# Sparse attention and feed-forward layer on one core: batch 1's K and Q in whole rows, batch 2 by natural loads and the crossbar, x of three batches by the crossbar

## The chip, the cores and the metric

The kernel runs on one core of a Trainium2 chip. The metric is the device time of one execution in microseconds (us). The core has TensorE (PE in the profile), VectorE (DVE), ScalarE (ACT), GpSimd (POOL) and SyncE (SP), which work beside each other and wait on semaphores, and 16 DMA engines that all transfers share.

## The reference

Attention over 4 batches, 8 heads, 768 positions and a head size of 64, with a band of 16 positions to each side and 24 summary keys (the maximum of each block of 32 keys, whose value is the block's mean), and then a feed-forward layer:

```python
k_sum = k.reshape(B, H, nb, block, D).max(axis=3)        # block = 32
v_sum = v.reshape(B, H, nb, block, D).mean(axis=3)
mask_l = np.abs(pos[:, None] - pos[None, :]) < window    # window = 16
scores_l = scale * (q @ k^T), -1e9 where not mask_l
scores_s = scale * (q @ k_sum^T) + np.log(block)
a = softmax(concat([scores_l, scores_s]))
x = (a @ concat([v, v_sum])).transpose(0, 2, 1, 3).reshape(3072, 512)
h = x @ w_in                                             # 512 x 2048
out = (h * np.clip(h + 3.0, 0.0, 6.0) / 6.0) @ w_out     # 2048 x 512
```

## The kernel before

The work is written as several hundred small operations, each with a tag, a number and an engine. `ORDER` is a text that lists all of them (`F30.0` is operation 0 of tag `F30`; `:A` or `:D` puts it on ACT or DVE where either can do it). A planner (`Plan.run`) goes through the text, gives each operation a begin from costs and due times written beside it, and the program is issued in the order of these begins. Within one engine that is the order of the text. On the chip each engine takes its operations strictly in that order and waits for what they need.

The tags: `K`, `Q`, `V` are loads that POOL issues (first digit the batch), `I` and `O` the parts of w_in and w_out, `h` the halo of V (the neighbouring 32 rows), `B` loads of V in blocks and `U` their sums on DVE. `k` and `q` bring K and Q into a layout with the head's 64 numbers across partitions, `w` makes the summary keys and the keys' halo, `s` is scores (matmuls on PE, the exponential on ACT, the mask's product on DVE), `u` block sums of V and their spreading, `v` the values. `v` with batch and 0 or 3 is one half of a batch: two groups of 24 small matmuls, a reciprocal and a product on DVE each, and then x turned so that the model dimension is across partitions. Half a batch is a tile s = 2b + half of 384 rows. `F` with tile and group is the first feed-forward product, 16 columns of 128 (operations 0 and 1 are four matmuls of 384 columns each, 2 is ACT's part, 3 DVE's); `G` with tile and 128-row part is the second product in four pieces of four matmuls of 512 columns, then a copy to `ot` and a store. Tile 0 is F0 and G0, and so on to 7. The halves of a batch come in the order 1, 0, so tile 3 goes ahead of tile 2.

Loads and turns before the change:

- Batch 0 has a path of its own, which the change leaves alone.
- Batches 1 and 2 (`load_raw`, line 450): K and Q come in 8 DMAs of 192 KB (in bf16) each, in which 32 of a head's 64 numbers go to one group of 32 partitions, so that each piece is half a row. `turn_raw` (608) turns them by 32x32 blocks on DVE, four operations for K and four for Q, into a layout with one head on 64 partitions. V's block sums come from matmuls (`vsum`, 745).
- Batch 3 (`load_nat`, 436): K and Q come in 12 natural loads of 128 rows (two of which are split in two DMAs) and are turned by four DMA transposes, the crossbar, issued by SP (`k_turn` 598, `q_turn` 589). V comes a second time in blocks (`load_blocks`, 727) and DVE sums it (`sum_blocks`, 732).
- Scores of batches 1 to 3 (`scores_all`, 666): six passes of 16 matmuls, each on 64 of the 128 rows, two heads at a time side by side.
- x (`values_half`, 825): tiles 2, 4, 5, 6 and 7 by the crossbar on SP; tile 3 (batch 1's half 1) by 12 PE transposes and three copies. After tile 2's turn POOL reads one number of it (`y10.0`, line 858), so that no load is issued before it has landed. Some F pieces of tile 3 are cut into thirds (`FINE`).
- Stores (`f2`, 941): SP issues them, except those of tile 5's part 1, which POOL issues.

A DMA that SP or POOL issues stands in that engine's queue behind what was listed before it, waits included. Buffers tie the steps: raw or natural K and Q of batches 2 lie in `both[0]`, those of 1 and 3 in `both[1]`; batch 3's V blocks lie in `both[0]`, so their loads wait until batch 2's K and Q have been turned. There are four `ot` buffers.

Of the kernel before, what the change touches and what calls it, by code (L numbers as in the profile page):

```python
# [12 lines left out]
F32 = mybir.dt.float32  # L13
# [5 lines left out]
D = 64  # L19
# [31 lines left out]
G12.4:A F33.4 G12.5 F30.7 F31.6 F33.5 y10.0 G01.5 F33.6 k21.0 F31.7 F33.0 F33.7 F33.1 h20.0 G31.0 Q32.0 F33.2 V30.0 F32.0  # L51
k20.0 F31.0 F33.3 F31.1 F31.2 k22.0 F32.1 F32.4 k23.0 F32.2 F32.5 F31.3 q23.0 G32.0 F32.6 Q33.0 F20.0 w2.3:A F32.3 F32.7
F20.1 G31.1 F20.2 G32.1 G32.2 F20.3 F21.0 q21.0 F21.4 q20.0 w2.4:A F21.5 F21.1 F20.4 w2.0 F21.6 F21.2 G31.2 G32.3 q22.0 V20.0
F20.5 G32.4:A F21.7 F20.6 F23.0 F23.1 w2.1 G31.3 w2.2:A F20.7 V22.0 G30.0 F21.3 h22.0 G30.1 F23.2 K31.0 s240.0 F23.3 s230.0
s250.0 G30.2 h30.0 G31.4:A s240.1 F22.0 F22.1 B33.0 G30.3 s250.1 s230.1 F22.2 V21.0 u2.0 q24.0:A s210.0 s220.0 F22.3 s200.0
G30.4:A s210.1 s240.2 s220.1 u2.1:D u2.8:D s250.2 s210.2 u2.2:D u2.9:A u2.4:A s230.2 s220.2 u2.7:D G20.0 F22.4 F22.5 F22.6
F23.4 G22.0 F23.5 G20.1 G22.1 F22.7 u2.3:D u2.6:D F23.6 F23.7 s200.1 v20.0 v20.3 s200.2 v20.4 v20.1 u2.5:D v20.2 v20.5 B31.0
K32.0 Q35.0 h31.0 K35.0 K33.0 Q31.0 V32.0 K34.0 B32.0 B30.0 h32.0 V31.0 Q34.0 Q30.0 V33.0 G21.0 G21.1 G22.2 G22.3 v23.3 v23.0
G20.2 G20.3 G21.2 G21.3 v20.6 G30.5 G21.4:A U3.2 v23.1 v23.4 U3.3 v23.2 U3.0 v23.5 F40.0 F40.1 F40.2 F41.4 F41.5 F41.6 F40.3
F41.7 G00.5 v23.6 q3x0.0 F41.0 F41.1 F41.2 F41.3 F42.0 F42.1 F42.2 G20.4:A F42.3 F40.4 F40.5 F40.6 F40.7 k3e0.0 G21.5 G32.5  # L60
# [12 lines left out]
G62.4:D G62.5 G71.2 G71.5 G71.8 G71.15 G71.16:A G71.17
# [199 lines left out]
def kernel(  # L273
# [42 lines left out]
    qs = {1: q1, 2: q2}  # L316
# [6 lines left out]
    raw = [{n: t[:, i * NS:(i + 1) * NS].rearrange("p u m -> p (u m)").rearrange("p (y c) -> p y c", c=BLK) for i, n in enumerate("KQ")} for t in both]  # L323
# [112 lines left out]
    def load_nat(b, name, u):  # L436

        plan.at(f"{name}{b}{u}")
        src, shift = (k, 0) if name == "K" else (q, PAD)
        n, lo = shift if u == 0 else 0, 128 * u - shift  # L440

        def go():
            o = nat[b % 2][name][:, u].rearrange("p (h d) -> p h d", h=H)
            if n:
                nc.gpsimd.dma_start(out=o[0:n], in_=src[b, :, S - n:S].rearrange("h r d -> r h d"))
            nc.gpsimd.dma_start(out=o[n:128], in_=src[b, :, lo + n:lo + 128].rearrange("h r d -> r h d"))
        op("POOL", 1.4 if n else 0.9, go, over=0.01, w=[(name + "n", b % 2, u)], dma=0.88, els=1024,
           free=[(name + "r", 1, g) for g in range(4)])

    def load_raw(b):  # L450
        for name, src in (("K", k), ("Q", q)):
            for g in range(4):
                plan.at(f"{name}{b}{g}")
                hs, ds, rows = slice(4 * (g // 2), 4 * (g // 2) + 4), slice(BLK * (g % 2), BLK * (g % 2) + BLK), slice(BLK * g, BLK * g + BLK)
                op("POOL", 1.35, over=0.01, fn=lambda src=src, name=name, hs=hs, ds=ds, rows=rows: nc.gpsimd.dma_start(  # L455
                    out=raw[b % 2][name][rows], in_=src[b, hs].rearrange("h (c r) d -> r (h c) d", r=BLK)[:, :, ds]),
# [640 lines left out]
```

## Time and profile before

| | us |
|---|---|
| median of 3 runs | 212.12 (211.94 to 213.3) |
| the profiled execution | 211.65 |
| its span, first to last instruction | 209.9 |
| PE busy | 201.7 |
| DVE busy | 156.0 |
| ACT busy | 110.8 |
| POOL busy | 68.9 |

The profile is of one execution. PE is matmuls and PEld weight loads, which overlap them. A view groups instructions by line, engine and operation: busy time, then the mean duration of one in ns, then the engine's idle time before them and what ended it. The chain of waits is followed back from the last instruction; its pieces have a start, a length and what they were. A stretch is a window of the span with each engine's busy time. The times to landing are from a DMA's issue to the end of its transfer.

### The profile page before, as it was taken

The numbers are of one execution on the slowest core, as the hardware profiler recorded it, in microseconds if no ns is written. First come the engines' busy times: TensorE is split into PE (matmuls) and PEld (weight loads), VectorE is DVE, ScalarE is ACT, GpSimd is POOL, SyncE is SP. The second block draws the span as 40 slices with busy tenths as digits, with TensorE's granted clock in tenths as the row PEclk, the third lists the DMA queues.
The fourth block names the chain that finished last, engine by engine and source line by source line (L and its number), as shares of the span: only waits on it lengthen the run. The fifth ranks groups of instructions, "written<-read, shape, count | busy, mean of one in ns | idle before, by whom it ended". The sixth has DMA issues, their size and how long they took to land.

```text
span 209.9 us, 5030 instructions
## 1 busy us (share of the span) xinstructions
PE 201.7 (96%) x2143; PEld 119.1 (57%) x2166; DVE 156.0 (74%) x229; ACT 110.8 (53%) x158; POOL 68.9 (33%) x89
## 2 busy tenths in 40 slices
PE   8999999999999999999999999999999999999993
PEld 2667876554455787455655466554554565665442
DVE  6898968997969989797599977899473756543212
ACT  5788576654389574547880166451990445623000
POOL 7572489626735603989840000000000100000000
PEclk9999999999999999999999999999999999999999
DMA  6999999999999999999995679900016310001055
GB/s 143 198 160 189 165 152 131 204 135 152 158 159 157 124 110 199 137 164 160 161 169 38 173 132 208 214 24 0 2 54 174 67 61 0 3 0 62 23 185 182
DMA packets 117638, 25.85 MB, mean 123 GB/s; under 512 B 108368, under 2 KB 114320, under 8 KB 117616
## 3 DMA queue, kind: packets, MB, share of 16 engines
q0 software_dynamic: 99488, 15.47, 106.8%
q1 hardware_dynamic: 18128, 10.06, 20.3%
q8 instruction: 17, 0.28, 0.6%
q14 instruction: 5, 0.04, 0.1%
HBM read 30.75 MB, written 6.29 MB: 176 GB/s over the span
## 4 chain that ended last, share of the span: by engine, by line
PE 60%; DMA 22%; POOL 5%; issue 5%; DVE 5%; ACT 2%; SPq 0%; POOLq 0%; ACTq 0%
PE S L928 28%; PE h L950 19%; PE S L950 9%; DMA vaug<-in_v_dram 9%; DMA wout<-in_moe_w_out_dram 5%; DMA win<-in_moe_w_in_dram 4%; DMA g<-in_q_dram 3%; PE S L841 2%; POOL nat L455 2%; DMA out_dram<-ot 2%; DVE at L689 2%; DVE g L936 1%; PE S L681 1%; DVE vaug L517 1%; ACT at L687 1%
## 5 line engine op out<-in xcount | busy, mean ns | idle before, releaser
L928 PE MATMUL S<-x,win 128*128 128x384 bf16 (+1 forms) x616 | 87.8, 299 | 0.4 <-ACT ot L517 0.3
L936 DVE SCALAR_TENSOR_TENSOR g<-r,S 128x768 bf16<-128x768 f32 x64 | 59.9, 948 | 24.5 <-ACT r L934 24.2
L934 ACT ACTIVATE r<-S 128x768 f32<-128x768 f32 x64 | 51.1, 810 | 46.0 <-PE S L928 42.0
L928 PEld LDWEIGHTS <-win 128*128 128x128 bf16 x616 | 53.6, 98 | 31.6 <-issue 0.8
L950 PEld LDWEIGHTS <-g 128*128 128x128 bf16 x416 | 38.7, 98 | 40.3 <-DVE g L936 0.4
L950 PE MATMUL h<-wout,g 128*128 128x512 bf16 (+2 forms) x256 | 58.6, 362 | 1.5 <-issue 1.0
L950 PE MATMUL S<-wout,g 128*128 128x512 bf16 (+1 forms) x139 | 30.0, 361 | 0.6 <-issue 0.3
L965 POOL DMA_DIRECT2D out_dram<-ot x1 | 0.6, 586 | 59.0 <-ACT ot L517 59.0
L687 ACT ACTIVATE at<-S 120x1024 bf16<-120x1024 f32 x18 | 17.9, 1023 | 1.6 <-PE S L681 1.4
L467 POOL DMA_DIRECT2D vaug<-in_v_dram x16 | 15.2, 949 | 6.4 <-issue 5.7
L517 ACT COPY ot<-h 128x512 f32<-128x512 f32 (+1 forms) x12 | 6.7, 558 | 18.4 <-PE h L950 16.9
L689 DVE TENSOR_TENSOR at<-at,mask 96x1024 bf16<-96x1024 bf16 x18 | 11.7, 683 | 1.6 <-ACT at L687 0.9
L455 POOL DMA_DIRECT2D nat<-in_k_dram x8 | 10.5, 1319 | 6.2 <-issue 4.7
L455 POOL DMA_DIRECT2D nat<-in_q_dram x8 | 10.6, 1329 | 3.3 <-issue 2.7
L782 DVE TENSOR_REDUCE red<-kb 128x48 bf16<-128x1536 bf16 x6 | 10.4, 1738 | 0.0
L517 DVE COPY ot<-S 128x512 f32<-128x512 f32 x5 | 3.5, 690 | 9.0 <-PE S L950 5.8
L517 ACT COPY ot<-S 128x512 f32<-128x512 f32 (+1 forms) x4 | 2.0, 502 | 14.8 <-DMA out_dram<-ot 10.0
L618 DVE STREAM_TRANSPOSE q<-nat 128x768 bf16<-128x768 bf16 x8 | 7.3, 956 | 2.8 <-issue 2.8
L521 DVE TENSOR_TENSOR vaug<-vaug 32x640 bf16<-32x640 bf16 (+2 forms) x21 | 7.7, 409 | 1.6 <-DMA vaug<-in_v_dram 1.2
L517 ACT COPY vaug<-vs 24x768 bf16<-24x768 bf16 x10 | 8.2, 827 | 0.2
L849 DVE TENSOR_TENSOR xm<-S,rc 128x768 bf16<-128x768 f32 x8 | 7.6, 954 | 0.2
L739 DVE TENSOR_REDUCE total<-nat 128x32 f32<-128x1024 bf16 x4 | 7.6, 1897 | 0.0
(105 smaller groups left out, 175.1 us busy)
## 6 DMA issues: line engine op xcount, KB each, us to landing
out_dram<-ot SPq DMA_DIRECT2D x18, 256.0 KB, 2.7
vaug<-in_v_dram POOLq DMA_DIRECT2D x16, 192.0 KB, 6.2
nat<-in_k_dram POOLq DMA_DIRECT2D x11, 192.0 KB, 6.7
win<-in_moe_w_in_dram POOLq DMA_DIRECT2D x4, 512.0 KB, 7.9
wout<-in_moe_w_out_dram POOLq DMA_DIRECT2D x4, 512.0 KB, 11.4
nat<-in_q_dram POOLq DMA_DIRECT2D x8, 192.0 KB, 13.6
out_dram<-ot SPq DMA_DIRECT2D x4, 224.0 KB, 3.3
g<-in_q_dram POOLq DMA_DIRECT2D x4, 192.0 KB, 5.9
```

The costliest lines, as they stand in the source:

```text
L455: op("POOL", 1.35, over=0.01, fn=lambda src=src, name=name, hs=hs, ds=ds, rows=rows: nc.gpsimd.dma_start(out=raw[b % 2][name][rows], in_=s ...
L467: op("POOL", 0.945, lambda: nc.gpsimd.dma_start(out=o[BLK:WIN, lo:hi, 0:D], in_=rows[:, lo:hi]), w=[("v", b % 2, c)], dma=1.28, els=1536). ...
L517: {"ACT": nc.scalar.copy, "DVE": nc.vector.tensor_copy, "POOL": nc.gpsimd.tensor_copy}[eng](o, i)
L521: nc.vector.tensor_tensor(o, i, i, op=ALU.max)
L687: op("ACT", 1.02, lambda: nc.scalar.activation(odds[0:KEYS, :, w], X.slot[0:KEYS], AF.Exp, scale=scl), r=[X], w=[("atg", k)])
L689: op("DVE", 0.69, lambda: nc.vector.tensor_tensor(odds[0:WIN, :, w].rearrange("p j (t c) -> p j t c", c=QB), odds[0:WIN, :, w].rearrange(" ...
L739: nc.vector.tensor_reduce(total[:, h * D + lo:h * D + lo + n], x[:, lo:lo + n], axis=AX.X, op=ALU.add)
L782: nc.vector.tensor_reduce(red.slot[:].rearrange("x (p u e n) -> x e u p n", p=NP, u=NS, e=2)[:, e], w[:, n * e:n * e + n, BLK:WIN].rearran ...
L928: nc.tensor.matmul(h.slot[:, f, u * 128:z * 128].rearrange("p (u c) -> p u c", c=128), w_in_sb[:, kt, (ft + f) * 128:(ft + f + 1) * 128], ...
L934: op("ACT", 0.81, lambda: nc.scalar.activation(r.slot[:], h.slot[:, :, 0:HALF], AF.Relu, bias=0.5, scale=1.0 / 6.0), r=[h], w=[r], alloc=r)
L936: op("DVE", 0.955, lambda: nc.vector.scalar_tensor_tensor(gt[s].slot[:, ft:ft + 2], r.slot[:], 1.0, h.slot[:, :, 0:HALF], op0=ALU.min, op1 ...
L950: nc.tensor.matmul(bank(o)[:, a:z], gt[s].slot[:, ft, ts * 128:(ts + 1) * 128], w_out_sb[:, ft, a:z], start=(ft == 0), stop=(ft == NFT - 1))
```

## The change

Batch 1's K and Q are loaded in whole rows, two heads to each group of 32 partitions, in 8 DMAs of half as many pieces; DVE turns them as before. A head's 64 numbers then lie in two places of the same 32 partitions, so the scores are sums of two products of 32 rows each, four heads at a time on the four strips of 32 rows (`scores_quarter`: four passes of 48 matmuls, each with two exponentials and two mask products of 768 columns). Batch 2 takes the path of batch 3: natural loads, four crossbar turns on SP, V's blocks summed by DVE. Tile 3's x goes through the crossbar like the other tiles. POOL issues the stores of tile 4, of tile 5's part 2 and of tile 6's part 1 too. `ORDER` is new from `K11.0` on. Some costs that the planner uses change with it.

```diff
 # ORDER, the stretch with batch 1's scores, cut
-h100.0:D h101.0:D G11.4:A G10.3 h130.0:D h131.0:D s120.0 G10.4:A G11.5 s110.0 s120.1 G02.3 G01.3 G00.0 h21.0 G02.4:A h110.0:D
-m.0 s110.1 G01.4:A s100.0 s150.0 s100.1 h111.0:D u1.0 u1.1:A K20.0 u1.6:A Q23.0 K22.0 s130.0 G00.1 G00.2 G00.3 Q21.0 K21.0
-s120.2 s100.2 u1.3:D u1.5:D u1.2:D s130.1 u1.7:A u1.9:D s110.2 s130.2 G12.0 v13.3 v13.0 v13.4 s150.1 K23.0 s140.0 v13.1 v13.2
-v13.5 u1.8:A K30.0 Q20.0 s140.1 G12.1 G12.2 v13.6 G12.3 s150.2 u1.4:A v13.7:A V23.0 s140.2 v13.10 v13.8 v13.11:D G00.4:A
-v10.0 v10.3 Q22.0 v13.9:D G02.5 v10.1 F30.0 v10.2 F30.1 F30.2 v10.4 v10.5 v10.6 F30.4 F30.5 F31.4 F30.3 F31.5 G10.5 F30.6
+G11.4:A q14.0:D K20.0 h120.0:A G02.3 s100.0 G02.4:A G02.5 K25.0 s100.1 h100.0:D Q22.0 h110.0:D G10.2 Q24.0 s100.3 h101.0:D
+G10.3 G10.4:A h121.0:D s100.2 K22.0 u1.0 u1.1:D u1.3:D s110.0 G01.3 s100.4 V21.0 s110.3 s110.1 u1.9:A G12.0 s120.0 G00.0
+G01.4:A G01.5 u1.5:D s120.1 u1.7:D B22.0 K23.0 s110.2 s110.4 v13.0 K21.0 v13.1 v13.2 u1.6:A u1.4:A v13.3 G00.1 V22.0 h20.0
+v13.4 v13.5 Q25.0 V23.0 s120.3 v13.6 G12.1 B20.0 s120.4 G12.2 s130.0 s130.1 u1.2:D s130.3 Q20.0 u1.8:A G00.2 G00.3 B21.0
+G00.4:A G12.3 s120.2 s130.2 s130.4 v10.0 v10.1 B23.0 v10.3 v10.4 v10.2 v10.5 v10.6 Q21.0 k2e0.0 y10.0 F30.0 F30.1 F30.2 F30.3
+Q23.0 F33.0 k2e1.0 F33.1 F33.2 q2x1.0 F31.0 F31.1 F33.3 F31.2 F31.3 F33.4 F33.5 F33.6 F33.7 F31.4 F31.5 F31.6 F31.7 F30.4
+F30.5 F30.6 F30.7 F20.0 F20.1 F20.2 F20.3 G12.4:A F32.0 F32.1 F32.2 F32.3 G32.0 q2x0.0 F21.0 F21.1 F21.2 h21.0 G10.5 B30.0
...
 # load_raw (batch 1 alone now)
-                hs, ds, rows = slice(4 * (g // 2), 4 * (g // 2) + 4), slice(BLK * (g % 2), BLK * (g % 2) + BLK), slice(BLK * g, BLK * g + BLK)
-                    out=raw[b % 2][name][rows], in_=src[b, hs].rearrange("h (c r) d -> r (h c) d", r=BLK)[:, :, ds]),
+                rows = slice(BLK * g, BLK * g + BLK)
+                    out=raw[b % 2][name][rows], in_=src[b, 2 * g:2 * g + 2].rearrange("h (c r) d -> r (h c) d", r=BLK)),
...
 # turn_raw reads a quarter of the rows' numbers at a time
+    def quarter(t, p):
+        return t[:, NB * (p // 2):NB * (p // 2) + NB, BLK * (p % 2):BLK * (p % 2) + BLK]
...
+    def scores_quarter(b, hh, half):
+        plan.at(f"s{b}{2 * (1 - half) + hh}0")
+        X = [Buf("S"), Buf("S")]
+        i, of = b % 2, (2 * hh, 2 * hh + 1)
+        def mms():
+            for n in range(HQ):
+                t = low(half) + n
+                for p in of:
+                    for g in range(4):
+                        rows = slice(BLK * g, BLK * g + BLK)
+                        nc.tensor.matmul(X[g // 2].slot[:, g % 2, QB * n:QB * n + QB], kb[i][rows, NP * NS * (t % 2) + NP * (t // 2) + p],
+                                         qs[b][rows, p, t * QB:(t + 1) * QB], start=p == of[0], stop=p == of[1])
...
+        for p, x in zip(of, X):
+            op("ACT", 0.81, lambda lo=lo, x=x: nc.scalar.activation(odds[0:KEYS, :, lo:lo + HALF], x.slot[0:KEYS, :, 0:HALF], AF.Exp, scale=scl),
+            op("DVE", 0.55, lambda m=m: nc.vector.tensor_tensor(m, m, mask ..., op=ALU.mult),
...
 # V's blocks of batch 2 lie in both[1], of batch 3 in both[0]
-        return both[0][32 * c:32 * c + NB]...
+        return both[b - 2 ^ 1][32 * c:32 * c + NB]...
-           free=[(n, 0, g) for n in ("Kr", "Qr") for g in range(4)])
+           free=[(n, 1, g) for n in ("Kr", "Qr") for g in range(4)] if b == 2 else [(n, 0, u) for n in ("Kn", "Qn") for u in range(NS)])
 # values_half
-        if b > 1 or b and not half:
+        if b:
 # f2
-            queue = "POOL" if (s, ts) == (5, 1) else "SP"
+            queue = "POOL" if s == 4 or (s, ts) in ((5, 1), (5, 2), (6, 1)) else "SP"
 # the batches' paths
-        if b < 3:
+        if b == 1:
             load_raw(b)
...
-        for i in range(6):
-            scores_all(b, i)
-        if b < 3:
+        if b == 1:
+            for half in (1, 0):
+                for hh in range(2):
+                    scores_quarter(b, hh, half)
             vsum(b)
         else:
+            for i in range(6):
+                scores_all(b, i)
             for c in range(NP):
                 load_blocks(b, c)
             sum_blocks(b)
```

More of the change, by code (lines that the diff above doesn't have):

```diff
@@ L52 @@
[L52 to L60, printed above, removed]
@@ L447, in load_nat @@
         op("POOL", 1.4 if n else 0.9, go, over=0.01, w=[(name + "n", b % 2, u)], dma=0.88, els=1024,
-           free=[(name + "r", 1, g) for g in range(4)])
+           free=[(name + "r", 1, g) for g in range(4)] + [("vb", 2, c) for c in range(NP)] if b == 3 else [(m, p) for m in ("kn", "qn") for p in range(NP)]
+           + [("kn", 1, j) for j in range(2)])
     def load_raw(b):
@@ L684, in scores_all @@
            + [("kh", b % 2, x) for x in range(2)] + [("kM", b % 2)],
-           w=[X], alloc=X, free=[("atg", k)] + ([("at", p, x) for p in range(NP) for x in range(2)] if b == 1 else []))
+           w=[X], alloc=X, free=[("ag", 1 - half, n) for n in range(4)])
         w = slice(n * QB * k, n * QB * (k + 1))
         op("ACT", 1.02, lambda: nc.scalar.activation(odds[0:KEYS, :, w], X.slot[0:KEYS], AF.Exp, scale=scl),
-           r=[X], w=[("atg", k)])
+           r=[X], w=[("ag", 1 - half, k % 3)])
         op("DVE", 0.69, lambda: nc.vector.tensor_tensor(
@@ L729, in load_blocks @@
         op("POOL", 0.8, lambda: nc.gpsimd.dma_start(out=rows_v(b, c), in_=v[b, 2 * c:2 * c + 2].rearrange("h (n r) d -> n h (r d)", r=BLK)),
[L730 removed]
+           w=[("vb", b, c)], dma=0.95, els=192, free=[(n, 1, g) for n in ("Kr", "Qr") for g in range(4)] if b == 2 else [(n, 0, u) for n in ("Kn", "Qn") for u in range(NS)])
     def sum_blocks(b):
@@ L737, in go @@
                 def go(h=h, lo=lo):
-                    x = both[0][:].rearrange("p u m -> p (u m)")[:, h * BLK * D:(h + 1) * BLK * D].rearrange("p (r d) -> p d r", r=BLK)
+                    x = both[b - 2 ^ 1][:].rearrange("p u m -> p (u m)")[:, h * BLK * D:(h + 1) * BLK * D].rearrange("p (r d) -> p d r", r=BLK)
                     nc.vector.tensor_reduce(total[:, h * D + lo:h * D + lo + n], x[:, lo:lo + n], axis=AX.X, op=ALU.add)
-                op("DVE", 1.92, go, r=[("vb", b, c) for c in range(NP)], w=[("vp", b, h, lo)])
+                op("DVE", 1.92, go, r=[("vb", b, c) for c in range(NP)], w=[("vp", b, h, lo)], free=[("vp", b - 1, h, lo)])
         op(EITHER, {"ACT": 0.265, "DVE": 0.25}, lambda eng: copy(eng, vs.slot[:], total[:]), r=[("vp", b, h, lo) for h in range(2) for lo in (0, n)],
@@ L842, in mms @@
                                          vaug[b % 2][0:KEYS, h, t, 0:D + 1], start=True, stop=True)
-            op("PE", 0.4, mms, form="values", r=([("atg", 3 * (1 - half) + k) for k in range(3)] if b else [("at", p, half) for p in range(NP)])
+            op("PE", 0.4, mms, form="values", r=([("ag", 1 - half, k) for k in range(4 if b == 1 else 3)] if b else [("at", p, half) for p in range(NP)])
                + [(m, b % 2, p, half) for m in ("vh", "vsum") for p in range(NP)] + [("v", b % 2, p) for p in range(NP)], w=[X], alloc=X)
```

85 lines of the change are left out of this document (50 added, 35 removed).

## The prediction

> **What bounds the kernel now.** I read the page first, then busy time by stretch, then the chain.
>
> ```profile
> span 209.9 us, 5030 instructions
> PE 201.7 (96%) x2143; PEld 119.1 (57%) x2166; DVE 156.0 (74%) x229; ACT 110.8 (53%) x158; POOL 68.9 (33%) x89
> 23.40:57.00 33.60, 33.49 (x229) 19.70 (x228) 28.84 (x36) 18.40 (x25) 22.29 (x24) 1.00 2.19 153
> 57.00:72.00 15.00, 14.14 (x290) 8.59 (x292) 12.81 (x27) 12.38 (x17) 8.11 (x8) 1.00 3.02 150
> 72.00:98.00 26.00, 25.84 (x225) 16.47 (x220) 23.54 (x27) 14.48 (x20) 15.72 (x20) 1.00 2.10 152
> 98.00:120.70 22.70, 21.79 (x326) 12.42 (x330) 18.83 (x28) 11.16 (x16) 8.53 (x11) 1.00 1.50 136
> 164.00:206.60 42.60, 42.44 (x258) 24.06 (x259) 20.31 (x25) 13.87 (x19) 0.59 (x1) 1.00 0.20 59
> ```
>
> The stretches list PE, PEld, DVE, ACT and POOL busy time, the granted clock (1.00) and the DMA share. From 23.4 us to the last matmul PE is never idle for more than a few per cent of a stretch, so a change pays there by taking work from PE or by ending one of its few waits. Before 23.4 us the two orders are the same. The rows that price PE's pieces come from the chain of waits (start, us, what) and from PE's timeline:
>
> ```profile
> 140.75 0.86 PE h L950 x4
> 141.61 0.65 PE S L928 x4
> 69.75 0.22 PE S L866 x4
> 70.84 0.45 PE S L866 x8
> 102.11 0.85 PE L752 MATMUL h<-vaug,ind 96*32 96x128 bf16 x48
> 102.90 0.87 PE L681 MATMUL S<-q,kb 64*128 64x64 bf16 x48
> L681 PE MATMUL S<-q,kb 64*128 64x64 bf16 x288 | 5.9, 191 | 0.1
> 72.10 1.07 PE L928 MATMUL S<-x,win 128*128 128x128 bf16 x16
> 205.70 0.91 PE h L950 x16
> ```
>
> An F piece (four matmuls) takes 0.65 us and a G piece 0.86. I added such durations along PE's part of ORDER, with 0.23 for a pass of scores, 0.35 for one of the new passes (both below), 0.46 for a values pass and 0.11 for each switch between kinds of matmul. For the kernel before, this puts F30.0 at 71.6 us (it ran at 72.10) and the last matmul's end at 205.4 (206.6). The 1.2 us between are PE's real waits. So the sum follows the trace, and I use it for the new order.
>
> **What the change takes from PE.** Batch 2's block sums leave PE: from 102.11 to the next pass at 102.90, 0.79 us. The PE transposes of x of tile 3 go: 0.22 + 0.45 = 0.67 us. No F or G piece is added or lost; one more switch costs 0.11. Fine F pieces stay (FINE is untouched).
>
> Batch 1's scores become 4 passes of 48 matmuls on 32-row strips, 192 instead of 96. In the 48-matmul row above one matmul lasts 0.19 us (the mean of L681's group), so starts are (0.87 - 0.19) / 47 = 14.5 ns apart, 29 ns for each pair of strips. If all four strips run in that round, a pass is 12 x 29 = 0.35 us and four are 1.40, what six passes of 8 x 29 cost now. If only two overlap, they are 24 x 29 x 4 = 2.8: +1.4. I take 0: the block sums above already run four 32-column strips, with starts (0.85 - 0.22) / 47 = 13.4 ns apart, where four undivided 128-column matmuls take 0.22 us, 55 each. PE's work is thus 0.79 + 0.67 - 0.11 = **1.35 us** less.
>
> The Trainium skill's page "TensorE: Matmul & The Clock Gate" (section "Wait — 56ns, not 53.3ns?") says that starts never come closer than about 25 ns; by it these passes would rise from 2.4 to 4.8 us, an estimate of +2.4. The trace disagrees with 14.5 and 13.4 ns.
>
> **What lies beside PE.**
>
> ```profile
> L687 ACT ACTIVATE at<-S 120x1024 bf16<-120x1024 f32 x18 | 17.9, 1023 | 1.6 <-PE S L681 1.4
> L517 ACT COPY x<-S 128x512 bf16<-128x512 bf16 x1 | 0.6, 586 | 0.2 <-PE S L866 0.2
> L658 ACT ACTIVATE at<-S 120x768 bf16<-120x768 f32 x8 | 6.2, 829 | 1.2 <-PE S L650 1.0
> L612 DVE STREAM_TRANSPOSE kb<-nat 128x768 bf16<-128x768 bf16 x8 | 7.5, 961 | 0.0
> L739 DVE TENSOR_REDUCE total<-nat 128x32 f32<-128x1024 bf16 x4 | 7.6, 1897 | 0.0
> L849 DVE TENSOR_TENSOR qwide<-S,rc 128x768 bf16<-128x768 f32 x6 | 5.5, 952 | 0.1
> L455 POOL DMA_DIRECT2D nat<-in_k_dram x8 | 10.5, 1319 | 6.2 <-issue 4.7 <-DMA nat<-in_q_dram 1.4
> L446 POOL DMA_DIRECT2D nat<-in_k_dram x6 | 5.4, 895 | 0.3 <-issue 0.3
> L729 POOL DMA_DIRECT2D nat<-in_v_dram x4 | 2.5, 622 | 0.9 <-DVE q L618 0.8
> L965 POOL DMA_DIRECT2D out_dram<-ot x1 | 0.6, 586 | 59.0 <-ACT ot L517 59.0
> L848 DVE RECIPROCAL rc<-S 128x12 f32<-128x12 f32 x14 | 2.8, 214 | 3.7 <-PE S L841 3.5
> ```
>
> Exponentials of batch 1: 8 x 0.83 against 6 x 1.02, +0.5 us on ACT, covered by 2.6 idle of its 15 us in 57 to 72 and by one 0.59 copy of x that goes. DVE in batch 2 loses eight transposes (8 x 0.96 = 7.7, Q's being of the same shape as K's) and gains four sums (4 x 1.90 = 7.6): nothing, though in 72 to 98 it is busy 23.5 of 26, so there is little cover for lateness. POOL's eight raw issues of batch 2 (8 x 1.32 = 10.6) become twelve natural ones (10.7) and four block loads (2.5); it has 10 us idle in the same stretch. Five more stores move from SP to POOL, which issues its only one now after 59 us of waiting; by then its loads are gone.
>
> SP gains five crossbar turns. These are the rows that matter most:
>
> ```profile
> L854 SPq DMA_TRANSPOSE x<-xm x3: 1379/1422/1439, 74.3 to 165.1; - x3
> DMA to landing us min/median/max: 3.6/3.8/7.6
> POOL seen L858 <- DMA x<-xm: 9.2, 1, 9.2
> 30.00:33.00 3.00, 3.00 (x20) 1.84 (x19) 2.31 (x4) 1.98 (x3) 3.00 (x4) 1.00 3.11 115
> 88.00:92.00 4.00, 4.00 (x25) 2.33 (x25) 4.00 (x4) 2.11 (x3) 3.13 (x5) 1.00 2.42 154
> 47.96 12.63 DMA vaug<-in_v_dram
> nat<-in_k_dram POOLq DMA_DIRECT2D x11, 192.0 KB, 6.7
> 60.62 1.09 DVE vaug L521 x3
> 61.26 0.23 PE L752 MATMUL S<-vaug,ind 96*32 96x128 bf16 x1
> 61.75 0.85 PE S L752 x47
> ```
>
> A turn lands 3.6 to 3.8 us after its issue in quiet; the one at 74.3, with loads ahead of it, took 7.6, though POOL held further loads back for it (9.2 us of waiting).
>
> Loads: raw pieces flow at 115 GB/s, whole natural rows at 154 (the last number of each stretch). One of 192 KB thus takes 1.7 us now and 1.3 after, 0.4 less. Batch 1 has eight, 3.2 us, and one 1.2 us halo load moves behind its V. V's last part, which lands at 60.6 and makes PE wait in its block sums (0.43 us between 61.26 and 61.75), lands near 56.2, its DVE copies end by 57.3, and the new sums are due at 58.6. I count that wait as gone: **-0.43**.
>
> **The step that may cost.** In the new order F30.0 stands at 71.1 us by the sum, and no G piece of tiles 0 and 1 is left ahead of it: G12.3, G10, G01 and G00 have all run. What it needs, x of tile 3, now comes from values v13 (last matmul 65.6), 0.2 us reciprocal, 0.95 scaling, and a turn issued near 66.9. Behind it on SP wait the turn of v10, the four of K2 and Q2, and the stores. POOL, meanwhile, loads batch 2 without a stop until its wait y10.0: eleven natural loads (0.85 each), three V, one halo and four blocks (1.3 each) from about 55.2 on, to 75. So the turn meets loads ahead and behind. Landing after 3.8 us gives 70.7, no wait; after 7.6, 74.5, a wait of 3.4. The nearest row is the loaded one, but those were pieces at 115 GB/s and these flow at 154; I take the middle, 5.7: 72.6, a wait of **+1.5**.
>
> The Trainium skill, "DMA: Bandwidth & Descriptors" (section "Queues, rings and completion order"), says that each DMA engine alternates between its queues packet by packet. Halving the turn's share, 3.8 - 1.4 = 2.4 us of transfer would become 4.8, so landing 6.2 and a wait of 2.0, an estimate; no run here shows it in this place.
>
> Three rows for what comes later: the landing of natural loads, that of K3's turns, and how long ACT waits for a free ot buffer.
>
> ```profile
> DMA to landing us min/median/max: 4.4/6.3/9.6
> DMA to landing us min/median/max: 4.8/5.0/5.2
> ACT ot L517 <- DMA out_dram<-ot: 10.0, 1, 10.0
> ```
>
> These steps have slack. v10's turn, issued near 72.2, has until F20.0 at 78.9 plus that wait. y10.0 frees POOL then; Q23 needs about 6 us to land, Q2's last turn about 5 (K3's took 4.8 to 5.2), near 92, against s250.0 at 93.5 plus the wait. Block loads of batch 3 reuse K2's and Q2's buffer and wait for that turn, V20 is queued behind them: it would land near 101, and v20 is due at 104.7. If these covers go, each costs PE its own delay.
>
> **Sum:** -1.35 - 0.43 + 1.5 = -0.3 us. The profiled execution took 211.65 us, 1.75 around its span; it is 0.47 below the median 212.12. The change of -0.3 on the median gives 211.8.
>
> **Rivals.**
>
> - *No new wait.* The turn lands like the quiet ones and the order hides everything, as the order before did but for 1.2 us. For: batch 1's loads are lighter. Then -1.8, 210.3; with all 1.2 us of waits gone, 1.35 + 1.2, 209.6. Against: the loads up to 75 us. Chance 0.32.
> - *The turn starves* (slower). Load packets keep the engines until about 75 us, and the turn follows with its 2.4: 77.4, a wait of 6.3. With -1.8 that is +4.5, 216.6. It passes 1% when the wait exceeds 3.9 us, a landing after 75.0. For: 7.6 us even though POOL was held; here it isn't. Against: that turn also moved while loads flowed. Chance 0.15.
> - *Strips overlap only in pairs*: +1.4 on the forecast, 213.2. For: no pass on 32-row strips is in the trace. Against: the four column strips. Chance 0.08. By the 25 ns of the Trainium skill's page "TensorE: Matmul & The Clock Gate" it would be +2.4, an estimate.
> - *The change does less than it says*: batch 2's turns are as late as its DVE transposes were, and a late Q23 or V20 costs what PE gained: 212 to 214. Chance 0.10.
>
> The forecast, a wait of 0.5 to 3.4 us, 210.8 to 213.7, has 0.35.
>
> **How the numbers follow.** About 1% (2.1 us) is what a measurement of this kernel can tell from no change. Faster than 210.0 needs the first rival with most of the other waits gone, half of its chance, or a PE gain that I haven't seen: 0.20. Slower than 214.2 is the starved turn and a part of the last two: 0.18. The rest, 0.62, lies within. The range, 209.5 to 214.8, takes in the best case and the forecast with strips in pairs, and leaves out most of the starved turn.
>
> **What would show it.** PE busy in total near 200.4 us, block sums once (x48) instead of twice, no transposes of qwide by PE; 192 strip matmuls of L681's kind in about 1.4 us plus switches, starts about 7 ns apart. The wait ahead of F30's first matmul, put down to the DMA x<-, is the term to read: 0, 1.5 or 6 us. The turn's landing should stand above 5 us. V1's landing should no longer be on the chain. It would all be wrong if the loads of batch 2 end well before 67 us, if DVE falls behind in batch 1 so that the scores themselves are late, or if SP's turns hold back stores until ACT waits for a free ot buffer, as it does for 10.0 us now near 110.

## The result, and the profile after

The changed kernel takes **225.3 us** (median of 6 runs, 224.5 to 227.9) against 212.0 for the kernel before on the same chip: a ratio of 1.065, with a 95% interval of 1.058 to 1.071. The forecast was 211.8, no change. The profiled execution is the longest of the six, 227.86 us, so its waits are rather longer than the median's. Here and below, ratios are of the executions within 1.5% of a kernel's fastest, medians and ranges of all.

First the page of after (busy time and TensorE's clock in 40 slices), then the same stretches as before, with PE, PEld, DVE, ACT and POOL busy time, the granted clock, the DMA share and GB/s:

```profile
span 226.1 us, 5152 instructions
PE 208.6 (92%) x2202; PEld 120.8 (53%) x2202; DVE 156.1 (69%) x227; ACT 110.5 (49%) x156; POOL 71.1 (31%) x103
...
PE   8899999999969259999999679999999999999994
...
57.00:72.00 15.00, 13.01 (x282) 6.81 (x278) 8.57 (x18) 9.45 (x15) 9.60 (x12) 0.89 2.13 179
72.00:98.00 26.00, 19.11 (x214) 13.95 (x213) 12.50 (x16) 9.95 (x14) 5.29 (x8) 0.87 1.43 149
98.00:120.70 22.70, 22.55 (x247) 12.09 (x245) 21.86 (x27) 15.66 (x19) 12.28 (x16) 1.00 1.22 114
120.70:147.00 26.30, 22.53 (x157) 11.99 (x155) 16.61 (x20) 8.60 (x11) 5.80 (x8) 0.87 1.79 163
```

The last of these stretches in the kernel before, which the prediction did not need:

```profile
120.70:147.00 26.30, 26.20 (x150) 14.73 (x151) 22.74 (x26) 13.15 (x17) 0.00 (x0) 1.00 0.55 115
```

PE, which was idle for 0.1 us in 120.7 to 147, is idle for 3.8 there, for 6.9 in 72 to 98 and for 2.0 in 57 to 72. And the granted clock is no longer 1.00: 0.89, 0.87 and 0.87 in those same three stretches. The waits of PE and POOL (us in total, times, longest) and the chain (start, us, what) name the places:

```profile
PE S L958 <- DMA x<-qwide: 10.7, 2, 6.9
PE S L710 <- issue: 2.0, 1, 2.0
POOL nat L446 <- DVE total L769: 10.4, 1, 10.4
```

```profile
61.96 0.41 PE S L710 x40
62.38 1.99 issue
64.36 0.24 PE S L710 x8
...
68.78 12.84 DMA x<-qwide
...
81.65 8.38 PE S L958 x78
```

```profile
121.60 9.98 DMA x<-qwide
131.57 0.05 issue
131.62 3.38 PE S L958 x10
```

What the reader is to see: the crossbar turn of tile 3's x, issued at 68.78, lands **12.84 us** later, and PE stands 6.9 us ahead of F30.0. The turn of tile 4's x takes 9.98, and PE stands 3.8 us. Between 62.38 and 64.36 PE stops in the midst of a score pass, after 40 of its 48 matmuls, and waits for nothing that the profile shows. Behind each of the three the matmuls themselves are slow. Behind tile 3's wait, 24 of 128 columns begin 107 ns apart in place of 56 and then 6 of 384 columns 320 ns in place of 162: 2.1 us over the normal distance. Behind tile 4's it is 18 of 384 columns, 2.8 us. Behind the stop PE first runs at its normal pace for 1.3 us; then 6 matmuls of 512 columns begin about 427 ns apart in place of 216 and a values pass is stretched, 1.5 us together. The granted clock is 0.50 for 3.4, 6.8 and 6.8 us at these places.

So PE loses 6.9 + 3.8 + 2.0 + 6.4 = 19.1 us, less the 1.35 of work that left it: 17.75. Its last matmul ends 16.6 later than before (223.2 against 206.6). The 1.1 us between fit the 1.2 us of short waits that the prediction counted in the kernel before; beside its three long ones PE stands only 0.15 us in after.

### The profile page after: what moved, and what is told of

The parts are those of the page before. It is cut to its first block, busy times and chain, and to the rows that moved or that the text cites. A ratio compares the mean times of both kernels' runs of the same rounds, so it can differ in the third digit from the quotient of the medians.

```text
span 226.1 us, 5152 instructions
## 1 busy us (share of the span) xinstructions
PE 208.6 (92%) x2202; PEld 120.8 (53%) x2202; DVE 156.1 (69%) x227; ACT 110.5 (49%) x156; POOL 71.1 (31%) x103
## 4 chain that ended last, share of the span: by engine, by line
PE 70%; DMA 15%; DVE 10%; issue 2%; POOL 1%; ACT 0%; DVEq 0%; POOLq 0%; ACTq 0%
PE S L958 35%; PE h L980 17%; PE S L980 10%; DMA x<-qwide 10%; DVE total L769 3%; DMA vaug<-in_v_dram 3%; DVE g L966 3%; DMA nat<-in_k_dram 2%; PE S L871 2%; DVE at L693 1%; DVE red L812 1%; PE S L685 1%; PE S L710 1%; PE h L732 1%; PE S L840 1%
## 5 line engine op out<-in xcount | busy, mean ns | idle before, releaser
L958 PE MATMUL S<-x,win 128*128 128x384 bf16 (+1 forms) x616 | 92.2, 310 | 10.7 <-DMA x<-qwide 10.7
L980 PE MATMUL h<-wout,g 128*128 128x512 bf16 (+1 forms) x272 | 63.4, 375 | 0.0
L980 PE MATMUL S<-wout,g 128*128 128x512 bf16 (+2 forms) x144 | 28.6, 350 | 0.0
L769 DVE TENSOR_REDUCE total<-nat 128x32 f32<-128x1024 bf16 x8 | 15.0, 1904 | 0.0
L691 ACT ACTIVATE at<-S 120x1024 bf16<-120x1024 f32 x12 | 11.5, 1023 | 2.8 <-PE S L685 2.8
L693 DVE TENSOR_TENSOR at<-at,mask 96x1024 bf16<-96x1024 bf16 x12 | 7.9, 683 | 4.0 <-ACT at L691 3.9
L717 ACT ACTIVATE at<-S 120x768 bf16<-120x768 f32 x8 | 6.1, 804 | 5.5 <-PE S L710 5.4
L878 DVE RECIPROCAL rc<-S 128x12 f32<-128x12 f32 x14 | 3.2, 228 | 7.7 <-PE S L871 7.6
L759 POOL DMA_DIRECT2D nat<-in_v_dram x8 | 4.8, 597 | 10.5 <-DMA q<-nat 9.0
L871 PEld LDWEIGHTS <-at 120*64 120x64 bf16 x336 | 6.5, 116 | 2.7 <-issue 2.0
```

The source lines that it names most:

```text
L691: op("ACT", 1.02, lambda: nc.scalar.activation(odds[0:KEYS, :, w], X.slot[0:KEYS], AF.Exp, scale=scl), r=[X], w=[("ag", 1 - half, k % 3)])
L693: op("DVE", 0.69, lambda: nc.vector.tensor_tensor(odds[0:WIN, :, w].rearrange("p j (t c) -> p j t c", c=QB), odds[0:WIN, :, w].rearrange(" ...
L769: nc.vector.tensor_reduce(total[:, h * D + lo:h * D + lo + n], x[:, lo:lo + n], axis=AX.X, op=ALU.add)
L871: nc.tensor.matmul(X.slot[64 * c:64 * c + 64, e, (D + 1) * y:(D + 1) * (y + 1)], odds[0:KEYS, j, u * QB:(u + 1) * QB], vaug[b % 2][0:KEYS, ...
L958: nc.tensor.matmul(h.slot[:, f, u * 128:z * 128].rearrange("p (u c) -> p u c", c=128), w_in_sb[:, kt, (ft + f) * 128:(ft + f + 1) * 128], ...
L980: nc.tensor.matmul(bank(o)[:, a:z], gt[s].slot[:, ft, ts * 128:(ts + 1) * 128], w_out_sb[:, ft, a:z], start=(ft == 0), stop=(ft == NFT - 1))
```

## The experiments

Theory: PE's losses come from crossbar turns that meet loads, and from PE standing still; the work itself costs what was predicted. Rivals: the new order is late as a whole; a turn is slow by itself; one cause is behind both waits.

**One part undone: tile 3's x on PE again.**

```diff
-        if b:                        # x by the crossbar
+        if b > 1 or b and not half:  # tile 3 by PE
 # ORDER: v13.6 to v13.11 (12 transposes, 3 copies) behind G12.2, s130.0 and G00.2
```

> After, with one thing undone: tile 3's x is turned by TensorE again (12 transposes, 3 copies) instead of the crossbar. Theory (the turn starves beside the loads, and the idle PE then runs at half clock): the wait of 7.1 us ahead of tile 3's first matmuls (74.56 to 81.65 in after) and the 6 matmuls at half pace behind it (about 1.0 us) go, the transposes come back (0.7 us): 225.3 - 7.1 - 1.0 + 0.7, so 217 to 219 us; tile 4's wait of 4.0 us and its slow stretch (2.9 us) stay. Rival 1 (the new order is late as a whole and the turn only happens to be what PE waits for): another wait of over 4 us stands at the same place, 222 us or more. Rival 2 (one cause: tile 4's wait is the first wait passed on): both go, 211 to 213 us.

219.4 us (217.7 to 221.3), 1.025 [1.016, 1.035] of before. PE's waits:

```profile
PE S L957 <- DMA x<-qwide: 3.3, 1, 3.3
PE h L979 <- issue: 2.3, 7, 1.3
PE S L709 <- issue: 2.1, 1, 2.1
```

The ratio is that of two executions of 217.7 us; the profiled one took 221.1. One wait for x is left, tile 4's, and the stop, here with a second one of 1.3 us. The first wait goes and the second stays: they have causes of their own.

**One part alone: before, with tile 3's x by the crossbar.** The diff is the same condition the other way round, in the kernel before.

> Before, with one part of the change: tile 3's x by the crossbar, PE's 12 transposes and 3 copies for it left out; order, batch 1 and batch 2 as before. Theory (a crossbar turn in this stretch, where loads run, costs PE a wait): a wait of 4 to 9 us appears ahead of tile 3's first matmuls, with some matmuls at half pace behind it: 215 to 221 us. Rival (the turn is harmless, the new order and batch 2's loads made it slow): it lands in 6 us or less, PE waits under 1.5 us, 211 to 213 us.

220.7 us, 1.038 [1.030, 1.045]. The chain and PE's waits:

```profile
70.14 9.22 DMA x<-qwide
```

```profile
PE S L927 <- DMA x<-qwide: 7.2, 1, 7.2
```

As the theory has it: neither the new order nor batch 2's new path is needed for the wait.

**The turn alone on the DMA engines.**

```diff
 # ORDER: POOL waits for tile 3's turn, then issues the loads that stood ahead of that wait
-V22.0 h20.0 v13.4 v13.5 Q25.0 V23.0 s120.3 v13.6 ... y11.0
+v13.4 v13.5 s120.3 v13.6 y11.0 V22.0 h20.0 Q25.0 V23.0
```

> After, with POOL made to wait for tile 3's turn before it issues V of slice 2, the last Q and halo loads and everything behind them, so that fewer loads run beside the turn. Theory (the loads beside it make the turn slow): it lands 4 to 7 us after its issue in place of 12.8 us, PE's wait ahead of tile 3 falls from 7.1 to between 0 and 2 us, and 217 to 221 us come out unless the loads, now about 5 us later, make batch 2's scores wait. Rival (1536 packets of a strided crossbar turn take this long by themselves, or the issue is what is late): it still takes over 9 us, PE waits 6 us or more, and the time is 225 us or above.

The turn is as fast as in quiet, and the kernel is no faster: 227.8 to 235.9 us, against 224.5 to 227.9 for after. The profiled execution is the one of 235.9. Two turns of its chain come first, then PE's longest wait; three stretches show the DMA rates (last number) of a turn alone, of loads in rows alone, and of a turn with loads of both kinds, rows and blocks:

```profile
69.69 3.77 DMA x<-qwide
...
91.08 16.11 DMA kb<-nat
```

```profile
PE S L957 <- DMA x<-xm: 9.0, 1, 9.0
```

```profile
71.00:73.00 2.00, 1.84 (x56) 0.99 (x55) 0.42 (x2) 1.00 (x2) 0.00 (x0) 1.00 1.07 204
77.00:80.00 3.00, 3.00 (x36) 2.35 (x35) 2.28 (x3) 1.98 (x3) 3.00 (x5) 1.00 2.30 147
91.00:97.00 6.00, 4.40 (x22) 2.77 (x23) 0.78 (x1) 1.29 (x2) 2.04 (x3) 0.50 1.65 79
```

A turn by itself moves 204 GB/s and lands in 3.77 us, so it is not slow by itself. The held loads then met the next turns: tile 2's x and K2's, which landed 15.0 and over 16 us after their issue. Together they moved 79 GB/s, less than the turn alone or row loads alone; block loads alone are in none of these stretches. The theory holds for the turn and failed for the time: it did not ask which turn the loads would meet next. Whether the execution of 227.8 us had the same wait was not traced.

**Which loads? Batch 2's block sums back on PE, without the block loads.**

```diff
                     scores_quarter(b, hh, half)
-            vsum(b)
         else:
             for i in range(6):
                 scores_all(b, i)
+        if b < 3:
+            vsum(b)
+        else:
             for c in range(NP):
                 load_blocks(b, c)
             sum_blocks(b)
 # ORDER: B20.0 to B23.0 and U2 out; V20.0, h22.0 behind h21.0; u2.0 on PE behind s230.1
```

> After, with one thing undone: batch 2's block sums are PE's again and its block loads of V are left out, so that batch 3's K and Q loads no longer wait for VectorE to have read these blocks. Theory (batch 3's loads, held up by those sums, run into tile 4's turn): POOL's wait of 10.4 us on VectorE's sums goes, tile 4's turn lands in 4 to 6 us in place of 10.0, PE's second wait falls from 4.0 us to under 1 and the slow stretch behind it (2.9 us) goes; the sums cost PE 0.8 us: 225.3 - 4.0 - 2.9 + 0.8, so 218 to 221 us, with the wait of 7 us ahead of tile 3 left as it is. Rival (the loads are late from tile 3's wait, not from the sums): the second wait stays over 3 us, 224 us or more.

217.3 us, 1.022 [1.014, 1.031]: the size was near, the reason wrong. POOL's wait on the sums goes, but the wait that vanishes on PE is the first one:

```profile
PE S L957 <- DMA x<-qwide: 3.5, 1, 3.5
```

Tile 3's turn lands in 4.1 us without the four block loads; tile 4's still takes 9.62. Batch 3's K and Q are issued from 96 us on in place of 108, but the loads behind them still flow when tile 4's turn is issued.

**Both undone** (tile 3's x on PE, block sums on PE; the two diffs together).

> After, with tile 3's x turned by TensorE and batch 2's block sums on TensorE, both as before the change. Theory (the two waits are separate, each from loads beside a crossbar turn): both waits and both slow stretches go, only the stop of 2.2 us inside a strip pass is left: about 225.3 - 8.1 + 0.7 - 6.9 + 0.8, so 210.5 to 214 us. Rival (new order late in other places too): 215 us or more, with a third wait of over 2 us.

220.7 us, 1.041 [1.033, 1.049]. A miss: since the block loads had been tile 3's trouble, undoing the crossbar on top gains nothing and gives PE its transposes back. Of the 3.4 us more than with the sums alone, 0.7 are these, and 1.6 are tile 4's wait, which was 5.1 us here with a landing of 11.27 and had 6.8 us at half clock behind it in place of 3.4; in the eight kernels here that have it, after among them, it lies between 3.3 and 5.1.

**Block loads: their bytes or their kind?** Two kernels, each with one edit of the block loads of batch 2:

```diff
-    out=rows_v(b, c), in_=v[b, 2c:2c + 2].rearrange("h (n r) d -> n h (r d)", r=BLK)
+    # first kernel: the same bytes in rows of 128 bytes on all partitions
+    out=both[1], 768 columns from 768 c on, in_=v[b, 2c:2c + 2].rearrange("h (t p) d -> p (h t) d", p=128)
+    # second kernel: 128 bytes of one partition and head
+    out=rows_v(b, c)[0:1, :, 0:64], in_=...[0:1, :, 0:64]
```

> After, with batch 2's four block loads of V (192 KB each, in pieces of 4 KB on 24 partitions) replaced by loads of the same bytes in rows of 128 bytes on all partitions; the block sums of batch 2 are then taken over the wrong numbers, with the same work. Theory (the kind of load matters: beside block pieces a crossbar turn and the loads together fall to 80 to 110 GB/s, beside rows they keep about 150): 140 GB/s or more flow while tile 3's turn waits and moves, it lands 7 to 10 us after its issue in place of 12.8, PE's wait is 1 to 4 us, and the time 218 to 222.5 us. Rival (the bytes ahead of the turn are what counts): the wait stays at 6 us or more, 224 us or above.

> After, with batch 2's four block loads cut down to 128 bytes of one partition and head each; the block sums of batch 2 are then taken over what lay in the buffer, with the same work on VectorE. Both theories: tile 3's turn lands in 3.6 to 5 us, PE's wait of 7 us ahead of it and the slow matmuls behind it go, 215.5 to 218.5 us; tile 4's wait of 3 to 5 us stays, since batch 3's loads still follow the sums. Against both (the loads have nothing to do with it, as the sums on TensorE made the difference): the wait stays, 224 us or more.

The second gave 215.7 us, 1.016 [1.006, 1.027], with tile 4's wait (3.4 us) and the stop (1.8) left; tile 3's turn landed in 4.4 us. The first gave 224.6, 1.060 [1.053, 1.068], with 5.9 us ahead of tile 3. The first row is PE's wait in the second kernel, the next two are the chain and a stretch of the kernel with rows, the last is the same stretch of after:

```profile
PE S L963 <- DMA x<-qwide: 3.4, 1, 3.4
```

```profile
67.58 10.53 DMA x<-qwide
```

```profile
72.00:76.00 4.00, 0.21 (x14) 0.19 (x7) 2.01 (x4) 0.00 (x0) 0.00 (x0) 1.00 3.39 156
```

```profile
72.00:76.00 4.00, 2.76 (x57) 1.60 (x56) 2.54 (x6) 2.17 (x4) 0.00 (x0) 1.00 1.44 109
```

The kind matters for the rate (156 against 109 GB/s while the turn moves), but it brings the landing only from 12.84 to 10.53 and the wait from 6.9 to 5.9: the theory had the rate, the rival the time, and its wait but for 0.1. Most of the wait is the bytes of the loads, whatever their kind. The packets counted from the trace show how, in the kernel with rows (loads, then turn, per us):

```
from 67 us   677 loads    0 turn     issued at 67.58
     69     1176          0
     71     1215          0
     72      444        393
     73      400        401
     74      412        411
```

In quiet the first packets of a turn run about 1.3 us after its issue and 800 in a us; here they begin 4.3 us after it, behind 3 us in which the engines serve loads alone, and then share one for one with the loads. It is not simply first come, first served: the four loads issued between 64 and 67.5 us, ahead of the turn, landed between 73.3 and 79.6, the last two of them behind the turn's 78.1. What sets the start of the turn's packets stays open.

**Tile 4: batch 3's V held until the turns have landed** (on the kernel with batch 2's sums on PE).

```diff
-            if b == 1:                       # POOL reads x: no load before the turn has landed
+            if b < 3:
 # ORDER: V30 to V33, h30 to h32 out of batch 3's K and Q loads and behind y20.0 and y21.0
```

> As the kernel with batch 2's sums on TensorE again, and batch 3's V and halo loads (9 issues on POOL) held until tile 4's and tile 5's turns have landed. Theory (loads in flight beside a turn are all there is to its lateness): tile 4's turn lands 3.6 to 5 us after its issue in place of 9.6, PE's wait of 3.5 us ahead of it and the slow matmuls behind it go, and nothing waits for V of batch 3, needed only 30 us later: 217.3 - 3.5 - 2.5, so 210.5 to 212.5 us, with the stop of 2 us inside a strip pass left. Rival (the K and Q loads that stay ahead of the turn are enough to make it late): PE still waits over 2.5 us there, 215 us or more.

213.2 us, 1.005 [1.002, 1.008], 0.7 above what was expected (nine executions from 212.1 to 214.0; three of 216.3, 218.6 and 1168.5 were not traced). The profiled one took 212.2, inside the expected range, with a stop of 2.7 us. PE's only long wait, and the landing of all six turns of x (min/median/max):

```profile
PE S L709 <- issue: 2.7, 1, 2.7
```

```profile
DMA to landing us min/median/max: 3.6/3.7/3.9
```

Loads put elsewhere on POOL take tile 4's landing from 9.6 to at most 3.9 and 4 us from the kernel's time. Loads in flight are what made that turn late.

**The slow matmuls: PE kept busy through the waits.**

```diff
+            if (s, ft, f) in {(3, 0, 0): 32, (4, 4, 0): 18}:   # matmuls of 512 columns, result unused
+                keep(32 or 18, h.slot)
```

> After, with useless matmuls (32 and 18 of 512 columns, about 7 and 4 us) put ahead of tile 3's and tile 4's first matmuls, so that PE works while it would wait. Theory (an idle PE is what halves its pace for the first matmuls behind each wait): the matmul pitch behind the waits is 162 ns from the first on in place of 320 ns, about 1.0 + 2.9 us less: 220.5 to 223 us. Rival 1 (the slow pace is set by something else than idleness, for instance the traffic): 6 and 18 matmuls still run at 320 ns, 224.5 us or more. Rival 2 (the gain ahead of tile 4 is eaten, as its turn lands at a time of its own): 1 us gained, 223.5 to 225 us.

223.5 us, 1.054 [1.046, 1.062]. The same two stretches in after and then in this kernel; the column with two decimals ahead of the DMA share is the granted clock:

```profile
81.60:98.00 16.40, 16.35 (x157) 12.35 (x157) 9.26 (x10) 7.77 (x10) 5.29 (x8) 0.86 1.25 173
131.60:147.00 15.40, 15.38 (x77) 8.31 (x78) 6.90 (x9) 6.38 (x8) 0.58 (x1) 0.81 1.38 175
```

```profile
81.60:98.00 16.40, 16.10 (x168) 11.66 (x166) 9.80 (x10) 8.27 (x11) 5.35 (x8) 1.00 1.21 183
131.60:147.00 15.40, 15.40 (x93) 8.93 (x92) 10.09 (x11) 7.99 (x10) 0.53 (x1) 1.00 1.16 203
```

In these stretches the clock stays at 1.00 and every matmul of 384 columns begins 162 ns after the last, with as much traffic. Idleness, not traffic, halves the pace. The gain in time is 1.8 us, less than the theory's 2.3 to 4.8 and at the edge of the second rival: the stop was 2.9 us in the profiled run, 0.9 longer, and a turn still lands when the loads let it, so that F30.0 began at 83.26 in place of 81.65.

Not every idle stretch does it. Behind the stop of 2.7 us in the kernel with held V, and behind the wait of 3.4 us in the kernel with next to no block loads, the clock stayed at 1.00. The clock records of the traces change only in steps of 3.41 us, and counted by these steps the cases part: where PE stood more than 1.8 us within one step, the next ran at half clock, and where it stood less than 1.6 us, the next did not; of three cases between (1.62, 1.62 and 1.80 us) one did. The stop of 2.7 us lay 1.58 and 1.17 us in two steps, the wait of 3.4 us 1.80 and 1.62. Half pace lasted until a step in which PE had hardly stood (0.33 us at most).

**The stop inside a pass: strips alone, then half as many matmuls.** Before, with batch 1's whole rows and strip scores alone (batch 1's part of the diff, with before's order and the new passes put where the old ones stood):

> Before, with another part alone: batch 1's K and Q in whole rows and its scores in 32-row strips; tile 3's x on PE, batch 2's loads, sums and order as before. Theory (the strips themselves cost nothing, four lie side by side): score passes of 96 matmuls take 0.35 us, as in after, and the time is 211 to 213.5 us, no change. Rival 1 (the strip passes run PE out of instructions: the 2.2 us stop inside a pass that waits on nothing in after): such a stop comes again, 213.5 to 216 us. Rival 2 (strips overlap only by pairs where the order differs): passes of 0.7 us and more, 213 to 215 us.

216.7 us, 1.020 [1.014, 1.027], by the first rival, and by a wait for VectorE that this order brought with it:

```profile
PE S L721 <- issue: 2.3, 1, 2.3
PE S L721 <- DVE qwide L890: 1.8, 1, 1.8
```

The stop is the same, without crossbar turns or block loads. Now half the products of each strip pass, on the kernel with both parts undone:

```diff
-                for p in of:
+                for p in of[:1]:
```

> As the kernel with both parts undone (tile 3's x and batch 2's sums on TensorE), with half of the contraction of batch 1's strip scores left out: each pass has 24 matmuls with 24 weight loads in place of 48 with 48. Theory (PE stops because it runs through some 500 instructions before the next 256 are fetched, and the strip passes shorten the time for that): the stop of 2.2 us inside a pass goes or falls under 0.5 us, and with 0.7 us less work the time is 2 to 3 us below the kernel with whole passes. Rival (the stop has to do with what the passes compute or where their results go, not with their number): it stays over 1.5 us and the time falls by at most 1 us.

215.9 us, 1.017 [1.008, 1.025], 4.8 below the kernel with whole passes, and no stop. That is more than the 2 to 3 expected; 2.1 is the stop and 0.7 the work. The traces show the rest: 3.4 us at half clock behind the stop in the kernel with whole passes and none here, and a wait for tile 4 of 4.6 in place of 5.1.

PE's fetches of instructions are transfers of 16,384 bytes, 256 instructions of PE, in the trace's DMA records (in after they come 251 recorded instructions apart on average). The sixth of them, against PE's instructions issued (matmuls and weight loads, as recorded):

```
kernel                      fetch begins at   PE stops at    next start after, us
before                          1628               -            -
after                           1677             1729          2.2
strips alone                    1724             1724          2.5
sums on PE                      1693             1729          2.2
half products                   1608               -            -
pass later (next paragraph)     1648               -            -
  its next fetch                1976             1985          1.35
```

PE stops at 1724 or 1729, or 256 further on, at 1985, and starts again 2.3 to 2.4 us after the fetch began. It runs dry: counted from multiples of 256, a fetch begins at 130 to 213 in before and after once 150 us are past, and at 328 to 449 in this stretch of loads, and the strip passes use up 96 instructions in half a microsecond. That the loads are what makes the fetch late is argued from this and not shown by itself; with next to no block loads the stop was still 1.8 us.

**A version that beats before?** The third pass put behind four G matmuls, on top of held V loads; then batch 2's V too; then all parts of the change with both holds:

```diff
 # 1: ORDER
-G12.0 s120.0 G00.0 G01.4:A G01.5 u1.5:D s120.1 u1.7:D ... s110.2 s110.4 v13.0 ... v13.3 G00.1
+G12.0 G00.0 G01.4:A G01.5 u1.5:D u1.7:D ... s110.2 s110.4 G00.1 s120.0 s120.1 v13.0 ... v13.3
 # 2: V22.0 h20.0 V23.0 and y11.0 out; behind Q21.0: y11.0 V22.0 h20.0 V23.0
 # 3: after, with the edits of 1 and 2, batch 3's hold, and B20 to B23 behind y11.0
```

> As the kernel with batch 3's V held, and the third strip pass put behind 4 of tile 0's projection matmuls (G00.1), so that PE issues fewer instructions before 62 us. Theory (the stop is an instruction fetch that comes too late for PE's pace): the stop falls from 2.0 us to under 1, and the time is 1 to 2 us below the kernel with only V held: 208.5 to 211 us. Rival (the fetch comes as late as PE lets it, the stop only moves): a stop of over 1.5 us stands in the pass or behind it, and the two kernels are within 0.5 us.

> As the kernel with batch 3's V held and the third strip pass later, and three of batch 2's V and halo loads (issued on POOL at 58 to 62 us) held until tile 3's turn has landed; POOL and the DMA queues are idle there anyway. Theory (loads in flight are what delays both the turn and PE's instruction fetches): the turn lands in 3.6 to 4.5 us in place of 6.3, PE's waits of 0.8 us on it and of 1.0 us on instructions go: 209.5 to 211 us, a little below before. Rival (the three loads are then late for batch 2's sums and values): PE waits over 1 us for V of batch 2, 212 us or more.

> After, with every part of the change kept (tile 3's x by the crossbar, batch 2's block sums on VectorE) and only the order mended: batch 2's block, V and halo loads (7 issues on POOL) held until tile 3's turn has landed, batch 3's V and halo loads until tile 4's and 5's have, the third strip pass later. Theory (loads in flight beside the turns and the instruction fetches are the whole loss): tile 3's turn lands in 4 to 5 us, PE's waits ahead of tile 3 and tile 4 are under 1.5 us each, none behind them at half pace, and the time is 210.5 to 213 us, that of before or up to 0.8 us (the block sums) below the kernel with the sums on TensorE. Rival (the change asks for more than order can give: batch 3's K and Q, in the buffer of the blocks, still come late enough to meet tile 4's turn): PE waits over 2 us for tile 4's x or for batch 3, 214 to 218 us.

The first gave 211.7 us and the second 212.3, both 1.000 [0.997, 1.004]: no version here beats before, and both missed the ranges expected, which ended at 211. In the first the stop moved to the next block, as its rival said, and shrank:

```profile
PE h L979 <- issue: 1.0, 1, 1.0
...
PE S L957 <- DMA x<-qwide: 0.8, 1, 0.8
```

The second has 0.4 us on instructions left, still 0.8 on the turn, and no gain in time. The third, with every part of the change kept, scattered between 216.8 and 228.7 us. In the profiled execution, 228.6, tile 3's turn landed in 5.21 us and PE no longer waited for tile 4's, but the seven held loads met tile 2's turn:

```profile
73.55 16.15 DMA x<-xm
```

```profile
PE S L957 <- DMA x<-xm: 9.2, 1, 9.2
```

```profile
74.00:90.00 16.00, 6.76 (x89) 5.51 (x87) 5.73 (x6) 4.80 (x6) 4.41 (x7) 0.78 1.81 98
```

98 GB/s for 16 us, again with block loads among them. Neither theory nor rival had that wait; the mechanism is the one shown, at a third turn. PE also stood 2.7 us because ACT waited for a store to free an `ot` buffer, a sign that the prediction had named. The execution of 216.8 us was not traced, so whether it had this wait is not known. Whether holding the blocks still longer would do is not tried.

## Why the prediction was wrong, point by point

- **What PE would save: right, as far as it was read.** Block sums stand once in batch 1 and no more in batch 2, and the strips overlap four deep. PE's timeline of after:

```profile
56.49 0.55 PE L710 MATMUL S<-q,kb 32*128 32x64 bf16 x48
58.80 0.85 PE L782 MATMUL h<-vaug,ind 96*32 96x128 bf16 x48
59.58 0.55 PE L710 MATMUL S<-q,kb 32*128 32x64 bf16 x48
```

  (0.55 - 0.19) / 47 is 7.7 ns between starts, and a pass of 48 takes 0.36 us; 0.35 was forecast. The 25 ns that the Trainium skill's page "TensorE: Matmul & The Clock Gate" ("Wait — 56ns, not 53.3ns?") gives as the least distance is not seen. The 0.43 us wait for V's last part is gone. PE was free for F30.0 at 74.76, where the sum had 71.1; the stop (2.0) and the half pace behind it (1.5) are 3.5 of these 3.7 us. PE's busy time came out at 208.6, not near 200.4; the half pace is in it.
- **The failed step: the wait ahead of F30.0, +1.5 with bounds of 0 and 3.4.** It was 6.9. The landing was taken as 5.7, the middle of a quiet 3.8 and a loaded 7.6; it was 12.84. The loaded row had POOL holding back all loads behind the turn, which the prediction noted and did not price. Without the hold, the bound was no bound: in the kernel before with tile 3's x on the crossbar, beside raw loads but with no hold right behind it, the landing was 9.22. The rival *The turn starves* had the mechanism and nearly the size (a wait of 6.3) and got 0.15. The size is partly luck: its landing, 77.4, and PE's need for x, 71.1, were both some 4 us too early.
- The Trainium skill's packet by packet rule ("DMA: Bandwidth & Descriptors", "Queues, rings and completion order") agrees with 400 loads to 401 turn packets in a us once the turn moves. Its estimate of a landing of 6.2 missed the 3 us of loads alone ahead of the turn's first packet, where the trace does not follow the rule. Beside block loads the rate falls as well.
- **"These steps have slack" failed for tile 4.** The text followed v10's turn, Q23 and V20, but not batch 3's loads, issued from 83 to 107 us before the change and from 108 to 126 behind the sums now, which met tile 4's turn: 3.8 us. The sums alone do not explain it: without them the loads were issued from 96 us on, and the V loads among them still met that turn.
- **Two terms were absent.** PE that has stood long enough runs at half pace for a while: 6.4 us. The Trainium skill's page "TensorE: Matmul & The Clock Gate" ("What's actually happening") states such a gate with a window of about 3.4 us; the clock here does change in steps of 3.41 us, but a stop of 2.0 us within one step was enough. And PE's instruction fetch: 2.0 us. The Trainium skill's page "Runtime: NRT & Kernel Launch" ("Instruction fetch mechanics") has the blocks of 256 instructions, which the trace shows, and calls the fetch mostly hidden, which it is not here.
- *Strips only in pairs* and *No new wait* did not come. With the turns nearly quiet, tile 3's x by the crossbar and the sums on PE, the order came out at 1.000 of before; what the sums on VectorE would add to that was not seen, as the one kernel with them had its new wait.

## What to carry to other kernels

Price a transfer that moves onto the path with what flows when it is issued: in the kernel with rows the loads went on alone for 3 us, then the packets alternated. Where the only loaded row of a trace has a hold in it, it is no upper bound. And an idle stretch of PE can cost more than its length, here when it filled about half of a clock step of 3.41 us or more, while a denser stretch of short matmuls needs its instructions fetched in time.

## What the runs showed of the hardware that was not expected

- A crossbar turn and loads with 4 KB block pieces among them moved 79 to 109 GB/s side by side, the turn alone 204, row loads alone 147, turn and row loads together 156.
- PE stopped for 2.0 to 2.9 us without a semaphore at the same recorded instruction, 1729, in after and in four kernels made from it, and 256 further on in a fifth; in five others it stopped at 1723 or 1724, for 0.9 to 2.5 us.
- Half pace followed when PE stood some 1.8 us or more within one 3.41 us step of the clock; 3.4 us spread over two steps did not bring it.
- Matmuls on four strips of 32 rows start 7.7 ns apart.
